# Clustered attention and dense layers: more buffers for the weight sums, recovery in a bank of its own, late weights on another queue

## The chip, the cores and the metric

The kernel runs on one core of a Trainium2 chip. The metric is the device time of the whole launch in microseconds, as the median of several runs. The engines are named PE (TensorE), DVE (VectorE), ACT (ScalarE), POOL (GpSimd) and SP (SyncE); SP and ACT also issue DMA transfers.

## The reference

```python
B, H, S, D = 4, 8, 768, 64               # 16 clusters for each head
q_assign = argmax(q_n @ c_n.T)           # q, k, centroids normalised
k_assign = argmax(k_n @ c_n.T)
scores = where(q_assign == k_assign, q @ k.T / 8, -1e9)
attn = softmax(scores) @ v               # in fp32
x = attn, heads joined                   # (4, 768, 512)
u = x + (x.T @ U @ V).T                  # U: 768 x 32, V: 32 x 768, mixes tokens
out = u + relu(u @ w_ch1) @ w_ch2        # 512 -> 2048 -> 512
```

U, V and the two weights come as 64-bit words, which hold numpy's float64; all else is fp32.

## The kernel before

There is one plan. Every piece of work is a Python function, `at(time, fn, ...)` gives it a place, and at the end the pieces are sorted by place and issued in that order; each engine executes its own instructions strictly in the order of issue (`keep_order`). A place is a number without unit. `M0` is the place at which the dense layers begin.

**Attention** (16 pairs of heads, 12 places each) comes first. It matters here only in that its last pairs, and the token mixing of the last batch (`mix_u`, `mix_sum`, `mix_v`), reach into the first places behind `M0`.

**Dense layers of batch 0**, places `M0` to `M0 + 32`: two halves of the tokens (`nh = 2`), 16 steps each. A step f is `gemm1` (12 matmuls into a bank `ps_h`), `after_gemm1` (ACT: Relu into `hh`, L605; DVE: the difference `hl`, L606) and `gemm2` (9 matmuls into three banks y). Each fp32 product is made of three products of high and low parts. The weights are in four groups of four steps, `wg[g]`.

**Loading weights** (`load_weights`, stages 0 to 3, eight steps a group; `stages` holds the places): `fetch` brings 64-bit words into one of two raw buffers (L151); `upper` (ACT, L159) and `join` (three DVE instructions, L169 to L172) turn them into fp32; stage 3 splits them into a high part (ACT, L190) and a low part (L191, on DVE in groups 2 and 3). Groups 2 and 3 are loaded during the first half of the dense layers, one step a place.

**Weight sums.** Batches 1 to 3 use a scheme with seven products instead of eight for 2 x 2 blocks, which needs four sums of weight blocks for each of eight pieces of the weights (n = 0 to 7: four groups, two matrices, one piece every 3.2 places from `M0 + 1.5`). `recover` adds low and high part again (ACT copies the low part into a bank `ps_r`, L652; DVE adds the high part and writes a temporary, L653); `combine` makes the four sums in place on POOL (L658 to L664); `split` divides each into high (ACT, L671) and low part (POOL, L672), in one of two buffers `o`; `store_sum` writes the buffer to DRAM, `wc` (L675). Unsummed blocks go there from the weights themselves (`store_block`, L642). Temporaries of pieces n and n + 1 lie in different places, except that 6 and 7 have the same one.

**Batches 1 to 3**, 28 places each: `seven1` and `seven2` do the seven products of the two matrices, with weights fetched back from `wc` (`fetch_w1` L762, `fetch_w2` L774); `after1`, `h_sums` and `h_halves` between them, `after2` behind (L875). Before a batch, `turn_half` transposes its tokens, `u_sums` (DVE, L748) makes four differences of token blocks, and `u_halves` (ACT L753 and L757, POOL L754 and L758) splits seven operands. After a batch, `join_up` adds the products together in eight additions of 768 columns (L902, DVE and POOL) and stores the output; these fall into the first places of the next batch.

**PSUM** in the dense stage: four banks in rotation for everything called with `work` (`ps_h`, the joins' `ps_t`, `ps_r`, transposes), and four more in the pool `ps_y`, in rotation too, three of which a half holds. In the seven-product stage `bank()` takes the two pools by turns.

All transfers but one kind go through SP's queue, which also executes in order and stands at a transfer until what it waits for is done.

Of the kernel before, what the change touches and what calls it, by code (L numbers as in the profile page):

```python
# [29 lines left out]
F32 = mybir.dt.float32  # L30
# [15 lines left out]
P = 128  # L46
# [50 lines left out]
    "mix":  (  3.36,   6.22,  15.04,  16.96),  # L97
    "g0":   ( 35.66,  38.22,  42.54,  52.94),
    "g1":   (-26.11, -21.73,  -20.5, -18.29),
    "g2":   (  -1.6,   -0.6,    0.3,    0.6),  # L100
    "g3":   (  6.25,    7.2,    8.1,    8.4),
}

spots = [0.66, -0.06, 1.8, 2.25, 1.26, 2.09, 2.97, 3, 3.49, 3.81, 4.58, 5.03]
# [13 lines left out]
def clustered_attention_moe(ctx: ExitStack, tc: tile.TileContext, qk, v, cen, moe_U, moe_V, w1, w2, out):  # L118
# [20 lines left out]
    def work(name):  # L139
        return ps_w.tile([P, 512], F32, name=name, tag="w")  # L140
# [2 lines left out]
    make_identity(nc, ident)  # L143
    u_scr = [dram.tile([P, NT, DM], F32, name=f"u_scr{b}") for b in range(B)]

    def fetch(srcs, n):

        step = srcs[0].shape[0]
        rw = raw.tile([P, 512], I64, name="rw")[0:step * len(srcs), 0:n]
        for i, src in enumerate(srcs):  # L150
            nc.sync.dma_start(out=rw[i * step:(i + 1) * step], in_=src)  # L151
        return rw

    def upper(rw):
# [23 lines left out]
    def load_weights(g, step, stage):  # L178

        k, i = divmod(step, 4)  # L180
        if stage == 0:
            parts[g, step] = fetch([(w1, w2)[k][g, :, i, :]], 512)
        elif stage == 1:
            parts[g, step] = upper(parts[g, step])
        elif stage == 2:
            parts[g, step] = join(*parts[g, step], g > 1)
        else:
            w = parts.pop((g, step))[2].bitcast(F32)
            hi, lo = wg[g][2 * k][:, i, :], wg[g][2 * k + 1][:, i, :]
            nc.scalar.copy(hi, w)  # L190
            (nc.vector if g > 1 or g == 1 and step in (1, 2, 3, 5) else nc.gpsimd).tensor_sub(lo, w, hi)  # L191
# [368 lines left out]
    def open_mlp():  # L560

        early.close()
        sb = pool["sb"] = ctx.enter_context(tc.tile_pool(name="msb", bufs=1, reuse_waits="tile"))
        pool["y"] = ctx.enter_context(tc.tile_pool(name="ps_y", bufs=4, space=PSUM, reuse_waits="tile"))
        wg[2].append(weight_tile(2, "w2l", sb))
        pool["u1"] = sb.tile([P, 2 * ND * HS], F32R, name="u1")
        turned[1] = [pool["u1"][:, k * ND * HS:(k + 1) * ND * HS].rearrange("p (d n) -> p d n", d=ND) for k in range(2)]
        pool["h"] = [sb.tile([P, 2, HS], F32R, name=f"hx{k}") for k in range(3)]
        pool["f"] = sb.tile([P, 2 * ND * S], F32, name="f")
# [38 lines left out]

    def gemm2(i, f):
        if f == 0:  # L610
            live["y", i] = [pool["y"].tile([P, 512], F32, name=f"y_{t}", tag="y") for t in range(HT)]
        y, (hh, hl) = live["y", i], live.pop(("h", i, f))
        _, _, w2h, w2l = wg[f // FG]
        for t in range(HT):
            ts = slice(t * P, (t + 1) * P)
            nc.tensor.matmul(y[t], hh[:, ts], w2h[:, f % FG, :], start=(f == 0), stop=False)
            nc.tensor.matmul(y[t], hh[:, ts], w2l[:, f % FG, :], start=False, stop=False)
            nc.tensor.matmul(y[t], hl[:, ts], w2h[:, f % FG, :], start=False, stop=(f == NF - 1))
# [26 lines left out]
    def temps(n):  # L645
        at = 3072 * (n % 2 == 0 or n > 5)
        return [pool["f"][:, at + 512 * j:at + 512 * j + 512].rearrange("p (a n) -> p a n", a=2) for j in range(4)]

    def recover(n, k, g, j):
        hi, lo = (blocks(k, g, part)[("A21", "A11", "A22", "A12")[j]] for part in range(2))  # L650
        ps = work("ps_r").rearrange("p (a n) -> p a n", a=2)
        nc.scalar.copy(ps, lo.bitcast(F32))  # L652
        nc.vector.tensor_add(temps(n)[j], ps, hi.bitcast(F32))  # L653

# [8 lines left out]
        else:  # L663
            nc.gpsimd.tensor_sub(f[3], f[3], f[2])  # L664

    def split(n, k, g, j):
        w = temps(n)[(1, 0, 2, 3)[j]]
        o = pool["f"][:, 5120:6144] if j % 2 else pool["f"][:, 2048:3072] if n < 6 else pool["rw"]
        o = live["o", n, j] = o.rearrange("p (a n) -> p a n", a=2)
        hi, lo = (o[:, :, part * 256:part * 256 + 256] for part in range(2))  # L670
        nc.scalar.copy(hi.bitcast(F32R), w)  # L671
        nc.gpsimd.tensor_sub(lo.bitcast(F32R), w, hi)  # L672

    def store_sum(n, k, g, j):
        nc.sync.dma_start(out=wc[k][g][:, :, slot[k][("S3", "S1", "S2", "S4")[j]], :], in_=live.pop(("o", n, j)))  # L675


    uc = {key: arena[:, 2 * XS + 1536 * s:2 * XS + 1536 * s + 1536].rearrange("p (h k n) -> p h k n", h=2, k=2)
          for s, key in enumerate(order[0])}
    w1s = [w0.rearrange("p k i n -> p (k i n)")[:, 3584 * k:3584 * k + 3584] for k in range(2)]  # L680
    spare, count = [], {"bank": 0, "f": 0}

    def pieces(x, n):
        return [x[:, k * n:(k + 1) * n] for k in range(x.shape[1] // n)]
# [4 lines left out]
    def open_sevens():  # L689

        pool["w2s"] = [[arena[:, 0:3584]], [arena[:, 3584:6144], wg[2][3].rearrange("p i n -> p (i n)")[:, 0:1024]]]
        pool["ys"] = [x.rearrange("p (d t n) -> p d t n", d=ND, t=2) for x in pieces(pool["f"], ND * S)]
        at_end = w0.rearrange("p k i n -> p (k i n)")[:, 7168:7936]
        spare.extend(pair(x) for x in (arena[:, 16896:17664], arena[:, 17664:18432], at_end,
                                       wg[2][3].rearrange("p i n -> p (i n)")[:, 1024:1792]))
        pool["st"] = rows.tile([P, HT, DM], F32, name="st", tag="R")
        ring = []
        for _ in range(2):
            pool["rw"] = raw.tile([P, 512], I64, name="rw").bitcast(F32)
            ring += pieces(pool["rw"][:, 0:768], HS)  # L700
        for _ in range(2):
            ring.append(raw.tile([P, 512], F32, name="rw_g")[:, 0:HS])
            ring.append(raw.tile([P, 512], I32, name="rw_t").bitcast(F32)[:, 0:HS])
        pool["ring"] = ring

    def free_rows():
        spare.extend(pair(x) for x in pieces(pool["u1"], 2 * HS))
# [11 lines left out]
    def ring():  # L719
        count["f"] += 1  # L720
        return pool["ring"][count["f"] % len(pool["ring"])]

    def bank():
        count["bank"] += 1
        ps = work("ps_p") if count["bank"] % 2 else pool["y"].tile([P, 512], F32, name="ps_q", tag="y")
        return ps[:, 0:HS]

    def fetch_half(b, h):
# [8 lines left out]
    def u_block(b, key):  # L737
        k, t = int(key[1]) - 1, int(key[2]) - 1
        return pool["ys"][1 - b % 2][:, 2 * k:2 * k + 2, t]

    def u_sums(b, key):

        live["t", key] = [ring() for _ in range(2)]
        for k, to in enumerate(live["t", key]):
            b11, b12, b21, b22 = (u_block(b, x)[:, k] for x in (B11, B12, B21, B22))
            one, two = {T1: (b12, b11), T3: (b12, b22), T2: (b22, live["t", T1][k]),
                        T4: (b21, live["t", T2][k] if key == T4 else None)}[key]
            nc.vector.tensor_sub(to, one, two)  # L748

    def u_halves(b, key):  # L750
        if key[0] == "B":
            hi, lo = uc[key][:, 0], uc[key][:, 1]
            nc.scalar.copy(hi, u_block(b, key))  # L753
            nc.gpsimd.tensor_sub(lo, u_block(b, key), hi)  # L754
        else:
            for k, x in enumerate(live["t", key]):
                nc.scalar.copy(uc[key][:, 0, k], x)  # L757
                nc.gpsimd.tensor_sub(uc[key][:, 1, k], x, uc[key][:, 0, k])  # L758

# [253 lines left out]
    for n_, (g, k) in enumerate((g, k) for g in range(NG) for k in range(2)):  # L1013
        c = M0 + 1.5 + 3.2 * n_
        for r in range(4):
            at(c + 0.4 * r, recover, n_, k, g, r)
            at(c + (0.9, 1.4, 1.75, 2.1)[r], combine, n_, r)
            at(c + (1.6, 2.0, 2.4, 2.8)[r], split, n_, k, g, r)
            at(c + (2.1, 2.5, 2.9, 3.3)[r], store_sum, n_, k, g, r)
        for r, name in enumerate(("A11", "A12", "A22")):  # L1020
            for half in range(2):
                x = 2 * r + half
                at((95 + 47 * k + 6 * x) if g == 0 else M0 + 1 + 4.1 * (n_ - 2) + 0.65 * x, store_block, k, g, name, half)

    at(M0 + 18, open_sevens)
    at(M0 + 31.3, free_rows)
# [2 lines left out]
    for b in range(1, B):  # L1029
        o = M0 + NF * nh + 28 * (b - 1)  # L1030
        if b == 1:
            fetched, turns, sums = (o - 13.9, o - 6.4), (o - 7.7, o - 5.4), o - 3.8
        else:
            fetched, turns, sums = (o - 20, o - 14), (o - 17.2, o - 9.7), o - 4.5
        for h in range(2):
            at(fetched[h], fetch_half, b, h)
            for d in range(ND):
                at(turns[h] + 0.4 * d, turn_half, b, h, d)
        at(sums - 0.45, u_halves, b, B11)
        for k, key in enumerate((T1, T2, T3, T4)):  # L1040
            at(sums + 0.25 * k, u_sums, b, key)
        for k, key in enumerate((T2, T3, T1, B21, T4, B22)):
            at(sums + 0.45 + 0.42 * k, u_halves, b, key)

        seq = [(1, 0), (1, 1), (1, 2), (2, 0), (1, 3), (2, 1), (1, 4), (2, 2), (1, 5), (2, 3),
               (1, 6), (2, 4), (1, 7), (2, 5), (2, 6), (2, 7)]
# [22 lines left out]
                for K in range(2):  # L1069
                    at(t + 7 * U + 0.01 * K, fetch_w2, (x - x % 2 + 2 + K) % 8, *slots)  # L1070
        if b < B - 1:
            for j in range(8):
                at(o + 28.4 + 0.65 * j, join_up, b, j)
    for K in range(2):
        for s0, s1 in ((0, 4), (4, 7)):
            at(M0 + 23 + K, fetch_w1, K, s0, s1)
# [35 lines left out]
```

## Time and profile before

| | |
|---|---|
| median of 3 runs | 1042.35 us (1042.16 to 1042.52) |
| the profiled execution | 1039.17 us, of which its span 1037.4 |
| PE busy | 963.4 us, 93% |
| DVE, POOL, ACT busy | 704.7, 620.7, 470.1 us |
| TensorE's granted clock, mean | 0.976 |
| DMA | 205.27 MB, mean 198 GB/s |
| dense layers of batch 0 | from 467 us to 660 us |

The rows of the profile name an engine, a line of the kernel, an operation and a tile. A row "A <- B" of the waits says that A sat idle until B released it: total us, times, longest. In the timeline a row is start, duration, engine, line, and in brackets the idle time before it with what ended it. In the windows, each engine's busy time in a stretch is followed by the granted clock (1.00 is full), the busy share of the DMA engines and the rate. A group of instructions has count, busy us, mean ns, and idle time before. SPq and ACTq are the queues that issue DMAs. Busy time of PE is modelled: matmuls overlap, so that a matmul's row is longer than the time until the next one starts.

### The profile page before, as it was taken

Reading aid. Unit: us, or ns where it says so; the run is one execution under the profiler, and the core shown is the slowest. Engines: PE = TensorE matmul, PEld = TensorE weight load, DVE = VectorE, ACT = ScalarE, POOL = GpSimd, SP = SyncE. Lnnn points to the kernel's source line nnn. Section 1 sums busy time; section 2 is a strip of 40 time slices with the busy share of each in tenths; the row PEclk is TensorE's granted clock in tenths of the full one; section 3 lists DMA queues with packets and bytes.
Section 4 is the critical chain, followed back from the end, with each engine's and each line's share of the span. In section 5 each row is a group of like instructions: output and inputs, shape, how many; then the busy total and the mean of one; then the engine's idle time right before and its main releaser. Section 6 shows DMA issues by size and latency. Waiting matters only on the chain.

```text
span 1037.4 us, 15318 instructions
## 1 busy us (share of the span) xinstructions
PE 963.4 (93%) x5368; PEld 786.2 (76%) x5368; DVE 704.7 (68%) x1298; ACT 470.1 (45%) x837; POOL 620.7 (60%) x477
## 2 busy tenths in 40 slices
PE   6999999999999999897877979999999999999997
PEld 3666665666667666556656768999999999999997
DVE  5797777777777766866667323565687656875767
ACT  4454654565556554553444343453333433334330
POOL 5467676888688877732444655653486533864431
PEclk9899999999999999998998999999999999999999
DMA  7754555656475635333887678577666876677743
GB/s 185 190 131 114 146 149 149 176 158 160 122 217 145 168 89 173 98 121 102 292 306 233 226 258 316 178 260 272 241 228 234 284 278 244 219 259 240 272 143 142
DMA packets 68028, 205.27 MB, mean 198 GB/s; under 512 B 8112, under 2 KB 25520, under 8 KB 63088
## 3 DMA queue, kind: packets, MB, share of 16 engines
q1 hardware_dynamic: 67568, 204.21, 62.2%
q8 instruction: 42, 0.69, 0.3%
q14 instruction: 34, 0.28, 0.1%
q10 hardware_dynamic: 384, 0.10, 0.0%
HBM read 131.07 MB, written 41.94 MB: 167 GB/s over the span
## 4 chain that ended last, share of the span: by engine, by line
PE 69%; DVE 13%; DMA 5%; issue 5%; ACT 4%; POOL 3%; SPq 0%; ACTq 0%; DVEq 0%; POOLq 0%
PE o_ps L487 11%; PE ps_max L440 7%; PE st L464 6%; PE st L466 5%; DMA wc<-f 3%; PE ps_q L855 2%; PE ps_q L857 2%; PE ps_q L856 2%; PE ps_p L791 2%; PE ps_p L793 2%; PE ps_p L792 2%; PE ps_q L793 2%; PE ps_q L792 2%; PE ps_q L791 2%; PE ps_p L855 2%
## 5 line engine op out<-in xcount | busy, mean ns | idle before, releaser
L479 POOL TENSOR_TENSOR T<-T,pr 128x768 f32<-128x768 f32 x120 | 226.6, 1888 | 46.2 <-ACT pr L469 19.3
L442 DVE TENSOR_REDUCE m<-ps_max 128x1 f32<-128x384 f32 x384 | 195.2, 547 | 82.6 <-PE ps_max L440 81.1
L469 ACT ACTIVATE pr<-st 128x768 f32<-128x768 f32 x192 | 154.4, 812 | 86.2 <-PE st L466 68.3
L487 PE MATMUL o_ps<-pr,vt 128*64 128x384 f32 x768 | 133.4, 498 | 0.1
L440 PE MATMUL ps_max<-arena 128*128 128x384 f32 x384 | 127.6, 383 | 6.3 <-DVE oh L356 2.5
L464 PE MATMUL st<-arena 128*128 128x384 f32 x384 | 105.3, 356 | 1.8 <-ACT pr L469 1.8
L440 PEld LDWEIGHTS ps_max<-arena 128*128 128x128 f32 x384 | 71.1, 193 | 44.9 <-issue 21.4
L487 PEld LDWEIGHTS o_ps<-pr,vt 128*64 128x64 f32 x768 | 53.1, 139 | 67.1 <-issue 60.8
L466 PE MATMUL st<-arena 97*128 97x384 f32 x384 | 99.9, 342 | 4.3 <-DMA arena<-mT 2.4
L479 POOL TENSOR_TENSOR T<-pr 128x768 f32<-128x768 f32 x30 | 56.5, 1884 | 64.9 <-ACT pr L469 64.9
L464 PEld LDWEIGHTS st<-arena 128*128 128x128 f32 x384 | 66.4, 190 | 17.7 <-issue 9.9
L466 PEld LDWEIGHTS st<-arena 97*128 97x128 f32 x384 | 70.6, 191 | 6.2 <-issue 4.5
L491 ACT COPY os<-o_ps 128x384 f32<-128x384 f32 x32 | 15.3, 479 | 105.8 <-PE o_ps L487 105.8
L791 PE MATMUL ps_p<-arena,w 128*128 128x384 f32 x178 | 59.9, 336 | 3.2 <-ACT ring L803 3.2
L672 POOL TENSOR_TENSOR f<-f 128x512 fp32r<-128x512 f32 x28 | 36.0, 1285 | 44.0 <-ACT f L671 42.1
L793 PE MATMUL ps_p<-arena,w 128*128 128x384 f32 x178 | 59.5, 334 | 0.0
L792 PE MATMUL ps_p<-arena,w 128*128 128x384 f32 x178 | 59.5, 334 | 0.0
L791 PE MATMUL ps_q<-arena,w 128*128 128x384 f32 x158 | 53.5, 339 | 0.0
L792 PE MATMUL ps_q<-arena,w 128*128 128x384 f32 x158 | 52.9, 334 | 0.0
L793 PE MATMUL ps_q<-arena,w 128*128 128x384 f32 x158 | 52.8, 334 | 0.0
L606 DVE SCALAR_TENSOR_TENSOR hx<-ps_h,hx 128x384 fp32r<-128x384 f32 x32 | 17.7, 552 | 46.9 <-ACT hx L605 46.9
L380 POOL TENSOR_TENSOR arena<-R,arena 128x768 fp32r<-128x768 f32 x18 | 34.5, 1924 | 13.2 <-ACT arena L375 7.6
(482 smaller groups left out, 2441.5 us busy)
## 6 DMA issues: line engine op xcount, KB each, us to landing
w<-wc SPq DMA_DIRECT2D x24, 1024.0 KB
w<-wc SPq DMA_DIRECT2D x24, 768.0 KB
rw<-in_w SPq DMA_DIRECT2D x32, 512.0 KB
wc<-f SPq DMA_DIRECT2D x28, 512.0 KB
arena<-wc SPq DMA_DIRECT2D x17, 768.0 KB
R<-in_qk SPq DMA_DIRECT2D x32, 384.0 KB
arena<-arena SPq DMA_DIRECT2D x32, 384.0 KB
arena<-arena SPq DMA_DIRECT2D x64, 192.0 KB
```

The lines of the kernel that those rows point to most:

```text
L440: nc.tensor.matmul(ps[:, 0:HS], x1[:, 0, g // 2, g % 2, t * P:(t + 1) * P], x1[:, 1, h, g % 2, :], start=True, stop=True)
L442: nc.vector.reduce_max(live["m2", i][:, h, u:u + 1], ps[:, 0:HS], axis=AX.X)
L464: nc.tensor.matmul(st[:, j, 0:HS], x1[:, 1, hk, j, ks], x1[:, 0, h, j, :], start=True, stop=False)
L466: nc.tensor.matmul(st[:, j, 0:HS], x2[0:97, 1, hk, j, ks], x2[0:97, 0, h, j, :], start=False, stop=True)
L469: nc.scalar.activation(pr, st[:, :, 0:HS], AF.Exp, scale=SCALE)
L479: eng.tensor_add(T, live["p", i, h, 0] if c == 1 else T, live["p", i, h, c])
L487: nc.tensor.matmul(o_ps[64 * j:64 * j + 64, 0:HS], vv[:, c, j, :], pr[:, j, :], start=(c == 0), stop=(c == NT - 1))
L672: nc.gpsimd.tensor_sub(lo.bitcast(F32R), w, hi)
L791: nc.tensor.matmul(ps, w[:, 0, k], u[:, 0, k], start=(k == 0), stop=False)
L792: nc.tensor.matmul(ps, w[:, 0, k], u[:, 1, k], start=False, stop=False)
L793: nc.tensor.matmul(ps, w[:, 1, k], u[:, 0, k], start=False, stop=(k == 1))
L855: nc.tensor.matmul(ps, w[:, 0], h[:, 0], start=(j == 0), stop=False)
```

## The change

Sums: `split` becomes `split_high` and `split_low`. The high part goes to one of six places of 512 columns in rotation (four for the last two pieces); two of the six are the buffers `rw_t` of the loading. The low part is written over the sum in its temporary. `store_sum` becomes two transfers, of high and low part, with rows of 256 values instead of 512. Their places move back by 0.3 to 0.4 or so. `recover` has a bank of its own, `ps_r`, as the fourth of the pool `ps_y`, whose banks are now named and no longer in rotation.

Loads: the weights of groups 2 and 3 are fetched on ACT's queue, the places of their stages change by a few tenths, and the blocks of group 1 are stored from `M0 - 9` and `M0 - 2.5` on, before from `M0 + 1` and `M0 + 5.1`.

Batches: `u_sums` makes one difference at a time, with places of their own, `u_halves` likewise; the eight additions of `join_up` move from 0.4 to 4.95 places (one every 0.65) to two at 0.02 and 0.1 and six from 5 to 5.9.

```diff
-    "g2":   (  -1.6,   -0.6,    0.3,    0.6),
-    "g3":   (  6.25,    7.2,    8.1,    8.4),
+    "g2":   ( -1.25,      0,    0.4,    0.7),
+    "g3":   (  6.75,      8,    8.4,    8.7),
...
-            nc.sync.dma_start(out=rw[i * step:(i + 1) * step], in_=src)
+            queue.dma_start(out=rw[i * step:(i + 1) * step], in_=src)
...
-            parts[g, step] = fetch([(w1, w2)[k][g, :, i, :]], 512)
+            parts[g, step] = fetch([(w1, w2)[k][g, :, i, :]], 512, nc.scalar if g > 1 else nc.sync)
...
-        pool["y"] = ctx.enter_context(tc.tile_pool(name="ps_y", bufs=4, space=PSUM, reuse_waits="tile"))
+        pool["y"] = ctx.enter_context(tc.tile_pool(name="ps_y", bufs=1, space=PSUM, reuse_waits="tile"))
+        pool["o"] = [raw.tile([P, 512], I32, name="rw_t").bitcast(F32) for _ in range(2)]
...
-            live["y", i] = [pool["y"].tile([P, 512], F32, name=f"y_{t}", tag="y") for t in range(HT)]
+            live["y", i] = [pool["y"].tile([P, 512], F32, name=f"y_{t}") for t in range(HT)]
...
+    def high_of(n, j):
+        f = pool["f"]
+        places = [f[:, 5120:5632], f[:, 5632:6144], *pool["o"], f[:, 2048:2560], f[:, 2560:3072]]
+        count["o"] += 1
+        return places[count["o"] % (6 if n < 6 else 4)].rearrange("p (a n) -> p a n", a=2)
...
-        ps = work("ps_r").rearrange("p (a n) -> p a n", a=2)
+        ps = pool["y"].tile([P, 512], F32, name="ps_r").rearrange("p (a n) -> p a n", a=2)
...
-    def split(n, k, g, j):
+    def split_high(n, j):
         w = temps(n)[(1, 0, 2, 3)[j]]
-        o = pool["f"][:, 5120:6144] if j % 2 else pool["f"][:, 2048:3072] if n < 6 else pool["rw"]
-        o = live["o", n, j] = o.rearrange("p (a n) -> p a n", a=2)
-        hi, lo = (o[:, :, part * 256:part * 256 + 256] for part in range(2))
-        nc.scalar.copy(hi.bitcast(F32R), w)
-        nc.gpsimd.tensor_sub(lo.bitcast(F32R), w, hi)
+        o = live["o", n, j] = high_of(n, j)
+        nc.scalar.copy(o.bitcast(F32R), w)
+
+    def split_low(n, j):
+        w = temps(n)[(1, 0, 2, 3)[j]]
+        nc.gpsimd.tensor_sub(w.bitcast(F32R), w, live["o", n, j])
 
     def store_sum(n, k, g, j):
-        nc.sync.dma_start(out=wc[k][g][:, :, slot[k][("S3", "S1", "S2", "S4")[j]], :], in_=live.pop(("o", n, j)))
+        to = wc[k][g][:, :, slot[k][("S3", "S1", "S2", "S4")[j]], :]
+        nc.sync.dma_start(out=to[:, :, 0:256], in_=live.pop(("o", n, j)))
+        nc.sync.dma_start(out=to[:, :, 256:512], in_=temps(n)[(1, 0, 2, 3)[j]])
...
-        ps = work("ps_p") if count["bank"] % 2 else pool["y"].tile([P, 512], F32, name="ps_q", tag="y")
+        tag = ("y_2", None, "ps_r", None, "y_0", None, "y_1", None)[count["bank"] % 8]
+        ps = pool["y"].tile([P, 512], F32, name="ps_q", tag=tag) if tag else work("ps_p")
...
-            at(c + (1.6, 2.0, 2.4, 2.8)[r], split, n_, k, g, r)
-            at(c + (2.1, 2.5, 2.9, 3.3)[r], store_sum, n_, k, g, r)
+            at(c + (1.9, 2.25, 2.6, 2.8)[r], split_high, n_, r)
+            at(c + (2.4, 2.7, 3.0, 3.3)[r], split_low, n_, r)
+            at(c + (2.8, 3.1, 3.4, 3.7)[r], store_sum, n_, k, g, r)
...
-                at((95 + 47 * k + 6 * x) if g == 0 else M0 + 1 + 4.1 * (n_ - 2) + 0.65 * x, store_block, k, g, name, half)
+                since = (95, 142, M0 - 9, M0 - 2.5)
+                at(since[n_] + (6 if g == 0 else 0.9) * x if g < 2 else M0 + 1 + 4.1 * (n_ - 2) + 0.65 * x,
+                   store_block, k, g, name, half)
...
-        at(sums - 0.45, u_halves, b, B11)
         for k, key in enumerate((T1, T2, T3, T4)):
-            at(sums + 0.25 * k, u_sums, b, key)
-        for k, key in enumerate((T2, T3, T1, B21, T4, B22)):
-            at(sums + 0.45 + 0.42 * k, u_halves, b, key)
+            for r in range(2):
+                at((o - 4.9 if b > 1 else o - 3.9) + (k + 0.5 * r) * (1 if b > 1 else 0.8), u_sums, b, key, r)
+        for key, when_ in ((B11, -4.95), (T1, -4.2), (B21, -3.7), (T2, -3.2), (B22, -2.7), (T3, -2.2), (T4, -1.2)):
+            at(o + when_ * (1 if b > 1 else 0.8), u_halves, b, key)
...
-            for j in range(8):
-                at(o + 28.4 + 0.65 * j, join_up, b, j)
+            for j, when_ in enumerate((0.02, 0.1, 5, 5.3, 5.1, 5.45, 5.6, 5.9)):
+                at(o + 28 + when_, join_up, b, j)
```

Here `o` is the place at which batch b begins; before, `sums` was `o - 3.8` for batch 1 and `o - 4.5` for the others.

More of the change, by code (lines that the diff above doesn't have):

```diff
@@ L144, in clustered_attention_moe, with fetch @@
     u_scr = [dram.tile([P, NT, DM], F32, name=f"u_scr{b}") for b in range(B)]
-    def fetch(srcs, n):
+    def fetch(srcs, n, queue=nc.sync):
         step = srcs[0].shape[0]
@@ L680, in clustered_attention_moe @@
     w1s = [w0.rearrange("p k i n -> p (k i n)")[:, 3584 * k:3584 * k + 3584] for k in range(2)]
-    spare, count = [], {"bank": 0, "f": 0}
+    spare, count = [], {"bank": 0, "f": 0, "o": 0}
     def pieces(x, n):
@@ L698, in open_sevens @@
         for _ in range(2):
[L699 to L704, printed above, removed]
+            ring += pieces(raw.tile([P, 512], I64, name="rw").bitcast(F32)[:, 0:768], HS)
+        ring += [raw.tile([P, 512], F32, name="rw_g")[:, 0:HS] for _ in range(2)]
+        pool["ring"] = ring + [x[:, 0:HS] for x in pool["o"]]
     def free_rows():
@@ L739, in u_block, with u_sums @@
         return pool["ys"][1 - b % 2][:, 2 * k:2 * k + 2, t]
[L741 to L748, printed above, removed]
+    def u_sums(b, key, k):
+        to = live["t", key, k] = ring()
+        b11, b12, b21, b22 = (u_block(b, x)[:, k] for x in (B11, B12, B21, B22))
+        one, two = {T1: (b12, b11), T3: (b12, b22), T2: (b22, live["t", T1, k]),
+                    T4: (b21, live["t", T2, k] if key == T4 else None)}[key]
+        nc.vector.tensor_sub(to, one, two)
     def u_halves(b, key):
@@ L755, in u_halves @@
         else:
-            for k, x in enumerate(live["t", key]):
+            for k in range(2):
+                x = live["t", key, k]
                 nc.scalar.copy(uc[key][:, 0, k], x)
@@ L1031, in clustered_attention_moe @@
         if b == 1:
-            fetched, turns, sums = (o - 13.9, o - 6.4), (o - 7.7, o - 5.4), o - 3.8
+            fetched, turns = (o - 13.9, o - 6.4), (o - 7.7, o - 5.4)
         else:
-            fetched, turns, sums = (o - 20, o - 14), (o - 17.2, o - 9.7), o - 4.5
+            fetched, turns = (o - 20, o - 14), (o - 17.2, o - 9.7)
         for h in range(2):
```

## The prediction

> **What bounds the kernel now.** I read the windows by stage first, then the starts of the hidden-layer matmuls in the timeline, then the chain and the waits of each half of that stage. Attention ends at 467 us; from there to about 660 the first batch goes through the dense layers (32 steps of `gemm1` and `gemm2`), while weights of groups 2 and 3 are loaded and the 32 weight sums are built; after 660 three batches run in the seven-product form.
>
> ```profile
> span 1037.4 us, 15318 instructions
> core 0: us, PE busy (x) PEld busy (x) DVE busy (x) ACT busy (x) POOL busy (x), PEclk, DMA share, GB/s
> 467.00:572.00 105.00, 82.76 (x376) 68.17 (x377) 71.33 (x118) 47.93 (x95) 44.79 (x36) 0.93 0.69 230
> 572.00:660.00 88.00, 77.16 (x382) 68.45 (x381) 27.88 (x42) 31.20 (x63) 52.73 (x41) 0.96 0.70 245
> 507.00:522.00 15.00, 12.42 (x57) 10.13 (x58) 12.84 (x21) 7.75 (x16) 8.91 (x7) 1.00 0.86 298
> 467.03 0.44 PE L597 MATMUL ps_h<-arena,w 128*128 128x384 f32 x1 [0.24 <-DVE arena L589]
> 591.79 0.33 PE L597 MATMUL ps_h<-u,arena 128*128 128x384 f32 x1
> 595.98 0.33 PE L597 MATMUL ps_h<-u,arena 128*128 128x384 f32 x1
> ```
>
> The first L597 row is the first matmul of step 0, and the windows are cut where step 0, step 16 and the end of step 31 fall. The other two rows are the first matmuls of steps 20 and 21: an undisturbed step takes 595.98 - 591.79 = 4.19 us, so 16 steps would take 67.0. The first sixteen took 105, the other sixteen 88. The windows' busy time of PE hides much of this, since it counts matmuls at a slow clock as busy. No engine is full: DVE 71.33 of 105, DMA 0.69.
>
> What stands between is seen in the longest pieces of the chain of each half, and in who waited for whom there:
>
> ```profile
> 515.09 4.66 DMA wc<-f
> 537.90 4.39 DMA wc<-f
> 557.78 5.33 DMA wc<-f
> 579.05 5.10 DMA wc<-f
> 593.65 4.03 DMA wc<-f
> 607.57 10.40 DMA wc<-f
> ...
> ACT f L671 <- DMA wc<-f: 16.7, 8, 4.2
> ACT rw_g L159 <- DMA rw<-in_w: 20.3, 7, 5.2
> PE ps_h L597 <- DVE f L653: 6.6, 3, 3.3
> ...
> ACT f L671 <- DMA wc<-f: 24.1, 5, 9.2
> DVE hx L606 <- ACT hx L605: 42.8, 10, 8.7
> PE ps_uT L734 <- DVE f L653: 6.4, 1, 6.4
> ...
> SPq L151 <- DVE ps_t L172: 43.7, 12, 9.9
> ```
>
> `split` (L671) has two buffers for hi and lo together; ACT, which executes in order, stands at L671 until the store from two sums ago has landed. Behind it in ACT's order is the Relu of L605, behind that DVE's L606, behind that `gemm2`. That is the whole tie: a store's landing time, which nothing needs, sets the pace of PE. PE also stands for DVE's L653, because `recover` takes its banks from the same four as the hidden layer. The last row is the sync queue (SP), standing at a weight load until the join two steps earlier has freed the raw buffer, with stores queued behind it.
>
> **The change part by part.**
>
> *Six high buffers, low part in place.* The instructions stay: 32 ACT copies, 32 POOL subtractions of the same 512 columns. A high buffer returns after six sums instead of two, and the store is 3.9 places of the plan behind it, some 3.9 x 6.6 = 26 us at today's pace (105/16 = 6.6), against a longest wait of 10.40: the ACT wait is gone. The low part now lies in the temporary, so `recover` of the next set but one waits for a store; that is 3.3 places, 22 us, later at the least, so it too is covered, except for set 7, which has the same temporaries as set 6. There DVE's L653 at place 23.9 stands for stores issued from 23.5 to 24.4, the last two behind the fetch of the second chunk of w1 on SP. Bounds: 0 to 10.40 (the row at 607.57, where such fetches stood ahead of a store); I take half, 5.2, since the fetch of the first chunk now goes out ahead of all stores of set 6. Behind that DVE add stands L606 of steps 24 and 25, and behind it PE.
>
> First half: the three store pieces, 4.66 + 4.39 + 5.33 = 14.4 us. Bounds: 0, if what is late next is as late; and what DVE allows. DVE does the same work afterwards, 71.33 us, and its best stretch (12.84 of 15, 0.86) would need 71.33/0.86 = 82.9, so 22.1 is the most. I take 14.4: by the counts below DVE is what is late next, and it leaves no more than a few us beyond.
>
> ```profile
> L169 DVE TENSOR_SCALAR ps_t<-rw_g 128x512 int32<-128x512 int32 x16 | 10.9, 682 | 0.0
> L170 DVE SCALAR_TENSOR_TENSOR ps_t<-rw_g,ps_t 128x512 int32<-128x512 int32 x16 | 11.1, 696 | 0.6
> L172 DVE SCALAR_TENSOR_TENSOR ps_t<-rw,ps_t 128x512 int32<-128x512 int32 x16 | 11.1, 696 | 0.5
> L191 DVE TENSOR_TENSOR w1l<-ps_t,w1h 128x512 fp32r<-128x512 f32 x4 | 2.8, 692 | 7.7 <-ACT w1h L190 7.6
> L653 DVE TENSOR_TENSOR f<-ps_r,arena 128x512 f32<-128x512 f32 x12 | 8.1, 683 | 7.2 <-ACT ps_r L652 7.2
> L606 DVE SCALAR_TENSOR_TENSOR hx<-ps_h,hx 128x384 fp32r<-128x384 f32 x16 | 8.8, 550 | 4.1 <-ACT hx L605 4.1
> L672 POOL TENSOR_TENSOR f<-f 128x512 fp32r<-128x512 f32 x28 | 36.0, 1285 | 44.0 <-ACT f L671 42.1 <-DVE hx L606 1.8
> ```
>
> Per step of the first half DVE does a join, a low part, a Relu difference and 4/3.2 = 1.25 recoveries: 0.682 + 0.696 + 0.696 + 0.692 + 0.550 + 1.25 x 0.683 = 4.17 us, just what PE needs for a step. POOL does 2.5 operations of 1.285 a step, 3.2 us, and has room.
>
> Second half: the pieces are 5.10 + 4.03 + 10.40 = 19.5, less the 5.2 of set 7, 14.3. But PE can't gain what it didn't lose: it idled 88 - 77.16 = 10.8 us, of which I leave a little over one to waits that stay, and its clock was 0.96, at most 0.04 x 88 = 3.5 more. So 9.5 to 13.0 is the room, 0 the other end; I take 9.5 and half of 3.5, 11.2.
>
> *A bank of its own for recovery.* `recover` leaves the four shared banks, so that `gemm1` no longer waits for L653: 6.6 us in the first half and 6.4 in the second, but these overlap the chain pieces above and are not added again. Its price: ACT's copy waits each time for DVE's add of the one before. The plan puts them 0.4 place, 1.7 us at 4.19 a place, apart, and copy and add need less, so 0 unless DVE is behind; the other end is the slower rival. The dense output has three fixed banks instead of four in rotation; `gemm2` of the second half begins two steps' pieces after the sums are read, so 0.
>
> *Late weights through ScalarE's queue.* Sixteen loads leave SP for ACT, 1.25 places ahead of their use instead of 1.
>
> ```profile
> L151 SPq DMA_DIRECT2D rw<-in_w x32: 327/334/1372, 107.4 to 556.5; - x32
> L217 ACTq DMA_DIRECT2D arena<-mT x18: 677/732/1286, 24.1 to 434.5; - x18
> L675 SPq DMA_DIRECT2D wc<-f x28: 512/513/1549, 492.3 to 638.3; - x28
> ```
>
> Issuing costs ACT 16 x 0.327 = 5.2 us at least and 16 x 0.732 = 11.7 at most (the only rows of ACT's queue), beside 105 - 47.93 = 57 idle: 0. The load's wait for the join of two steps ago is now in ACT's order, but L190, which needs the same join, stands right ahead of it, so it holds nothing longer: 0. The gain is that stores on SP no longer stand behind it, and that loads no longer stand behind stores. ACT stood 20.3 us for loads; if all that went, the first half would reach DVE's limit of 22.1 and the sum below would be 1001.9. The page "DMA: Bandwidth & Descriptors" of the Trainium skill (Issuing engines are not separate DMA queues) speaks against this: all issuing engines' transfers run on the same 16 DMA engines, and another queue saves only time on the sequencer; by it the 14.4 stands and with it 1009.6. The row of the busy stretch, DMA 0.86 at 507 to 522, points the same way, and I take nothing for faster loads.
>
> *Stores in two pieces.* SP issues 32 more, 32 x 0.513 = 16 us over 193: hidden. Bytes are the same, the rows half as long. Two bounds: a row costs by its bytes, 0; or by its number, which is a rival below. Six to nine stores of group 1's blocks move ahead of 467 us, where DMA has room: a little better, 0.
>
> *Differences and joins spread.* At the two later batch borders PE waits thus (all of 657 to 1037, five groups):
>
> ```profile
> PE ps_p L791 <- ACT ring L803: 3.2, 2, 1.6
> PE ps_p L855 <- DVE f L875: 2.5, 2, 1.2
> PE ps_q L855 <- DVE f L875: 2.2, 2, 2.0
> PE ps_q L855 <- ACT acc L873: 1.9, 1, 1.9
> PE ps_q L855 <- DVE acc L875: 0.9, 2, 0.5
> ...
> L902 DVE TENSOR_TENSOR f<-f,acc 128x768 f32<-128x768 f32 x12 | 13.3, 1131 | 0.1
> ```
>
> Together 10.7 us. The 1.6s, the 2.0 and the 1.9 (7.1) come in the first three products of a batch, where DVE has about 12 operations of L606's size, 0.55, in each 7 us and four joins of some 1.1 on top. Six of the eight joins now come at 5 to 5.9 places, where second products begin and DVE has four adds instead of twelve. The other 3.6 come where the differences of the tokens stand in a row ahead of L875; these are spaced out. Bounds: 10.7, or below nothing, if joins bunched in 0.9 place delay the adds there by their 4 x 1.1 twice, -9. I take 7.1, the joins' share.
>
> **The sum.** 14.4 + 11.2 + 7.1 = 32.7 us off the span of 1037.4. The profiled execution took 1039.17 in all, the median of the runs is 1042.35, 3.2 above it; against the median the forecast is 1042.35 - 32.7 = 1009.6.
>
> **The rivals.**
>
> *More, as all ties go.* First half to DVE's 82.9 (22.1), second with its clock (13.0), both borders clean (10.7): 45.8, so 996.5. For it: the recovery bank gives PE two steps of lead. Against: 86% was DVE's best in 15 us, not in 80. On the clock, the row below shows a matmul of 0.54 us, where the same took 0.33 at 591.79, after 2.82 us of standing. "TensorE: Matmul & The Clock Gate" of the Trainium skill (What's actually happening) has the clock halved after some 3.4 us idle; the trace agrees (0.93, 0.96 in these windows), and by it fewer gaps give the time twice.
>
> ```profile
> 478.51 0.54 PE L597 MATMUL ps_h<-arena,w 128*128 128x384 f32 x1 [2.82 <-DVE f L653]
> ```
>
> *DMA becomes the bound.* If a half row costs as much as a whole one, 18 stores of the first half add 18 x 0.52 MB at 230/0.69 = 333 GB/s, 28 us, to 0.69 x 105 = 72: 100 of 105, a gain of 5 at most; 14 stores add 21 to 62 in the second: 83 of 88, again 5. With the borders 17, so 1025. Against it is a stretch with more than half its packets under 2 KB, which moved 294/0.805 = 365 GB/s:
>
> ```profile
> DMA packets 2167, 2.94 MB, mean 294 GB/s; under 512 B 125, under 2 KB 1379, under 8 KB 2166
> ...
> q1 hardware_dynamic: 2166, 2.94, 80.5%
> ```
>
> *Slower: the single recovery bank.* If DVE is behind, ACT's next copy stands for the add of the one before, and with ACT stand Relu and joins. The price is a join (2.07 us) at each of the 20 recoveries of the first half, 41 us: 1051. It decides from 32.7/20 = 1.6 us a recovery. For it: DVE's 4.17 in a step of 4.19, and bursts of four. Against: ACT has 57 idle us to catch up, and PE has a step in hand.
>
> *Nothing comes of it.* The store wait moves from ACT to DVE's L653 in every set, not set 7 alone: about 1042. Against: 22 us of distance.
>
> **How the numbers follow.** Forecast 0.48 (its own range 1000 to 1019), more 0.17, DMA-bound 0.20, nothing 0.05, slower 0.10. A measurement here tells about 0.2%, 2 us, from no change. Faster 0.85, same 0.05, slower 0.10. The range 990 to 1033 takes the forecast and nearly all of the two cases beside it.
>
> **What would show it.** Right: no ACT wait for `wc` stores left but some at the end; L606's wait for L605 under 15 us; steps of 4.3 to 5.5 us; DVE over 80% in the first half; one wait of L653 for a store near step 24; L803's wait at the borders gone. Wrong: ACT's copy for recovery waiting for L653 over 1 us on the mean, DMA share near 1.0 with lower GB/s, loads still awaited 20 us, or new waits of L875 behind joins at 5 places.

## The result, and the profile after

| | before | after |
|---|---|---|
| median | 1042.26 us | 1025.18 us (1025.03 to 1025.75) |
| ratio | | 0.9837, 95% interval 0.982 to 0.9854 |
| span of the profiled execution | 1037.4 us | 1024.0 us |
| step 0 to step 16 of the dense stage | 105.1 us | 92.7 us |
| step 16 to the first product of batch 1 | 83.9 us | 75.9 us |
| from there to the end | 381.3 us | 388.3 us |

The change makes the kernel 17 us faster, 1.6%. By the spans of the two profiled executions it is 13.4 us: that of before lay 3.1 us below its median, that of after 0.6 above. By these spans the dense stage gives 12.4 + 8.0 = 20.4 us, and batches 1 to 3 take 7.0 of it back. The cuts are these matmuls of the timeline: step 16 and the first product of batch 1 in before (step 0 is at 467.03), then step 0, step 16 and the first product in after. Batch 1 begins at 656.08 in the kernel before, not at 660.

```profile
572.16 0.34 PE L597 MATMUL ps_h<-u,w 128*128 128x384 f32 x1
656.08 0.34 PE L791 MATMUL ps_p<-arena,w 128*128 128x384 f32 x1
```

```profile
467.14 0.45 PE L598 MATMUL ps_h<-arena,w 128*128 128x384 f32 x1 [0.23 <-DVE arena L590]
559.80 0.34 PE L598 MATMUL ps_h<-u,w 128*128 128x384 f32 x1
635.68 0.34 PE L799 MATMUL ps_p<-arena,w 128*128 128x384 f32 x1
```

The windows of after, cut there (columns as in the windows of before):

```profile
467.00:560.00 93.00, 80.20 (x378) 64.95 (x379) 68.77 (x114) 47.19 (x92) 43.78 (x35) 0.96 0.73 238
560.00:636.00 76.00, 72.59 (x362) 63.99 (x361) 31.09 (x45) 32.56 (x65) 54.44 (x42) 0.98 0.81 284
636.00:1024.00 388.00, 367.26 (x2073) 362.60 (x2071) 264.51 (x469) 140.13 (x302) 190.39 (x173) 0.98 0.65 231
```

The waits of the dense stage of after (line numbers have moved, and move by one or so between the runs: here L606 is the Relu, L607 its difference, L659 recovery's copy, L660 its add, L676 the copy of the high part):

```profile
DVE hx L607 <- ACT hx L606: 27.2, 13, 7.5
ACT ps_r L659 <- DVE f L660: 22.3, 16, 8.3
...
DVE f L660 <- DMA wc<-f: 12.3, 3, 8.0
...
ACT rw_g L159 <- DMA rw<-in_w: 4.8, 2, 3.8
...
ACT rw_t L676 <- DMA wc<-f: 0.9, 1, 0.9
```

ACT's 16.7 + 24.1 + 9.2 us of waiting for stores have become 0.9, and its 20.3 for raw words 4.8. DVE's new wait for stores is there, in three pieces. In the DMA columns, the first half moves 238/0.73 = 326 GB/s at full share against 230/0.69 = 333 before, the second 284/0.81 = 351 against 245/0.70 = 350: with the stores in rows of half the length the rate fell by about 2% in one half and not at all in the other.

The waits of PE behind 630 us are the surprise:

```profile
PE ps_q L863 <- DVE rw L838: 6.1, 2, 3.0
PE ps_q L863 <- DVE ring L838: 4.0, 2, 2.0
PE ps_q L863 <- DVE rw_t L838: 3.9, 3, 2.0
PE ps_p L863 <- DMA arena<-wc: 1.1, 2, 0.6
```

The five groups at the borders of before are all gone, as forecast. In their place `seven2` (L863) stands for `h_sums` (L838), 14.0 us in seven waits, in all three batches and also in batch 1, where no joins fall. One of them in the timeline, with a later piece of what follows:

```profile
729.46 0.44 PE L863 MATMUL ps_q<-u,arena 128*128 128x384 f32 x1 [3.03 <-DVE rw L838]
...
731.07 0.67 PE L863 MATMUL ps_q<-h,arena 128*128 128x384 f32 x1
731.54 0.52 PE L864 MATMUL ps_q<-h,arena 128*128 128x384 f32 x1
```

Some 1.6 us after the wait of 3.03 us matmuls of the same shape take 0.52 to 0.67 us instead of 0.34: the wait is paid for again in clock. This holds for four of the seven. Windows of 3.3 to 3.4 us behind the waits of 1.98, 3.03, 2.04 and 3.03 us have a clock of 0.50; behind the other wait of 2.00 us, and those of 0.68 and 1.20, it stays at 1.00. The last of the four, and the 2.00:

```profile
860.40:863.70 3.30, 3.30 (x11) 3.20 (x12) 1.09 (x2) 0.34 (x1) 0.17 (x1) 0.50 0.02 5
828.00:831.40 3.40, 3.40 (x20) 3.40 (x21) 2.04 (x5) 0.98 (x2) 3.04 (x4) 1.00 0.00 0
```

Four such stretches at half clock lose about 4 x 3.4 x 0.5 = 6.8 us.

`h_sums` reads three results of `seven1` straight from their PSUM banks, late in the plan. A product that gets such a bank has to wait for it. In the kernel before, the second pool of banks hands out the bank whose last use comes first in the plan; in the programs' own bank numbers that pool begins batch 1 with 2, 1, 0, 3, 2, 3, 1, 0, 2, 3. The changed kernel names the banks, and `bank()` takes them in the cycle 3, 0, 1, 2 throughout, whether they are still to be read or not.

### The profile page after: what moved, and what is told of

Read it like the earlier page. It is cut to its first block, busy times and chain, and to the rows that moved or that the text cites. A ratio compares the mean times of both kernels' runs of the same rounds, so it can differ in the third digit from the quotient of the medians.

```text
span 1024.0 us, 15360 instructions
## 1 busy us (share of the span) xinstructions
PE 962.9 (94%) x5368; PEld 785.0 (77%) x5368; DVE 709.2 (69%) x1298; ACT 471.5 (46%) x837; POOL 624.1 (61%) x477
## 5 line engine op out<-in xcount | busy, mean ns | idle before, releaser
L849 POOL TENSOR_TENSOR h<-ring,h 128x384 fp32r<-128x384 f32 x21 | 21.5, 1031 | 36.0 <-ACT h L848 19.5
L607 DVE SCALAR_TENSOR_TENSOR hx<-ps_h,hx 128x384 fp32r<-128x384 f32 x32 | 17.7, 553 | 27.4 <-ACT hx L606 27.2
## 6 DMA issues: line engine op xcount, KB each, us to landing
w<-wc SPq DMA_DIRECT2D x24, 1024.0 KB
arena<-wc SPq DMA_DIRECT2D x10, 1024.0 KB
```

## The experiments

Theory A: the fixed cycle of named banks takes back what the rest brings. Its rival: the new places of differences and joins delay `h_sums`. Theory B, for the dense stage: the store wait of two buffers, and PE's wait for recovery's banks, set its pace, and the queue of the loads is worth nothing. Its rivals give the gain to one of these alone, or to the queue. Ratios are to the kernel before on the same chip, with 95% intervals. The runs were spread over several chips, on which the median of the kernel before was 1039.4 to 1042.3 us, so between chips the ratios are the better comparison. Code cuts are shortened.

**e1_rotating: the pool in rotation again, everything else changed.**

```diff
-tile_pool(name="ps_y", bufs=1, ...)
+tile_pool(name="ps_y", bufs=4, ...)        # y, ps_r and ps_q all with tag="y"
-        tag = ("y_2", None, "ps_r", None, "y_0", None, "y_1", None)[count["bank"] % 8]
+        ps = work("ps_p") if count["bank"] % 2 else pool["y"].tile(..., name="ps_q", tag="y")
```

> The changed kernel with one thing put back: the four banks of ps_y (three dense outputs, recovery, every second product of batches 1 to 3) are one pool in rotation again, which hands out the bank that the plan releases first, instead of four named banks in a fixed cycle. Theory (the fixed cycle is where the gain went: seven waits of L863 for L838, 6.1 + 4.0 + 3.9 = 14.0 us, and the half clock that follows them): these waits go and nothing else moves, the part behind the first L799 falls from 388.3 us to some 371 to 374, 1009 to 1012 us in all. Rival (the new places of differences and joins cost the time, by delaying the sums L838): the waits of L863 for L838 stay, 1022 to 1026.

Measured: 1005.86 us, 0.9676 (0.9652 to 0.9699). The part behind the first product takes 1003.4 - 634.6 = 368.8 us, 19.5 less than in the changed kernel and 12.5 less than before; the dense stage is as it was (92.9 and 74.3). All waits of PE in that part, and its window:

```profile
PE ps_q L862 <- DVE f L882: 1.8, 2, 1.6
PE ps_q L862 <- ACT acc L880: 1.2, 1, 1.2
PE ps_p L862 <- DMA arena<-wc: 0.4, 1, 0.4
```

```profile
635.00:1003.00 368.00, 359.32 (x2072) 356.64 (x2070) 256.52 (x469) 139.97 (x302) 192.03 (x173) 1.00 0.68 244
```

The waits for `h_sums` are gone, the clock is 1.00. Waits fell by 11.7 us (15.1 to 3.4), the time by 19.5; the other 7.8 are what 388 us at 0.98 instead of 1.00 come to, and the four stretches at half clock are 6.8 of them. The gain is more than the theory's 1009 to 1012. By the ratios (0.9837 to 0.9676) it is 17 us.

**e2_named_alone: the kernel before with named banks and nothing else.**

```diff
-        ps = work("ps_p") if count["bank"] % 2 else pool["y"].tile([P, 512], F32, name="ps_q", tag="y")
+        tag = ("y_2", None, "y_3", None, "y_0", None, "y_1", None)[count["bank"] % 8]
+        ps = pool["y"].tile([P, 512], F32, name="ps_q", tag=tag) if tag else work("ps_p")
```

> The kernel before with one thing of the change alone: the four banks of ps_y are named and go round in a fixed cycle; recovery still takes its bank from the shared four. Theory (the fixed cycle costs the time): waits for h_sums (L830 in the kernel before, L832 or so here) of about 14 us appear in batches 1 to 3 beside the 10.7 us that are there, 1053 to 1060 us. Rival (places of differences and joins): no such waits, 1041 to 1044.

Measured: 1054.17 us, 1.0144 (1.0122 to 1.0167). Its waits of PE behind 655 us begin thus, above those of before:

```profile
PE ps_q L856 <- DVE rw L831: 6.1, 2, 3.0
PE ps_q L856 <- DVE rw_t L831: 5.0, 3, 2.4
PE ps_q L856 <- DVE ring L831: 4.0, 2, 2.0
PE ps_p L792 <- ACT ring L804: 3.2, 2, 1.6
```

Seven waits again, 15.1 us, without any of the new places, and 1.4% or 15 us more time. With e1 this settles A. Its dense stage is that of before but for the names of the banks, and that of e3 is the same code; the first half takes 108.1 us here and 108.6 in e3, against 105.1 in the profile of before. So this half varies by some 3 us between executions.

**e3_spread_alone: the kernel before with the new places of differences, splits and joins** (the last two hunks of the diff and `u_sums` for one half at a time).

> The kernel before with one part of the change alone: the places of the token differences, of the operand splits and of the joins. Theory (they do what was forecast, and the loss lies elsewhere): the 10.7 us of waits at the two later borders go, with some us of half clock behind them, 1029 to 1035 us. Rival (the new places cost more than they bring): 1042 to 1050.

Measured: 1029.64 us, 0.9909 (0.9882 to 0.9935). From the first product (657.94) to the end (1026.5) 368.6 us, 12.7 less than before; of the waits at the borders 2.6 us are left.

**e8_old_joins: as e1, the joins at their old places.**

```diff
-            for j, when_ in enumerate((0.02, 0.1, 5, 5.3, 5.1, 5.45, 5.6, 5.9)):
+            for j, when_ in enumerate(0.4 + 0.65 * x for x in range(8)):
```

> As e1_rotating, but with the eight joins at 0.4 to 4.95 places as before; the differences stay spread. Theory (the joins bring about two thirds of what the borders gained): waits of some 7 us of the kind 'L798 for L810' and 'L862 for L882' return, 1013 to 1017. Rival (the differences bring it): under 3 us, 1005 to 1008.

Measured: 1013.56 us, 0.9753 (0.9718 to 0.9788), about 7.7 us above e1. The three waits of before that were put down to the joins are back:

```profile
PE ps_p L798 <- ACT ring L810: 3.2, 2, 1.6
PE ps_q L862 <- DVE f L882: 2.2, 2, 2.0
PE ps_q L862 <- ACT acc L880: 1.9, 1, 1.9
```

**e4_rotating_sp_loads: as e1, the late weights on SP's queue.** In `load_weights`, `nc.sync` for all groups.

> As e1_rotating, but the weights of groups 2 and 3 are loaded through SP's queue again, at the new places. Theory (the other queue only takes the loads out of SP's order; loads and stores share the engines that move them): ACT's waits for raw words rise from 4.8 us towards the 20.3 of before, the first sixteen steps are 0 to 6 us longer than with ACT's queue, 1009 to 1017 in all. Rival (the queue is what brought the first half its 12 us): over 10 us longer, 1019 to 1025.

Measured: 1003.27 us, 0.9656 (0.9631 to 0.9681), the same as e1 within the intervals. ACT's wait for raw words is 4.1 us, not towards 20. So with the new places either queue brings the loads in time, and that part of the expectation was wrong.

**e7_old_load_places: as e4, and the stages of the loads at their old places too.**

> As e4_rotating_sp_loads, but with the places of the load stages of groups 2 and 3 as before the change too, so that nothing of the change to the loads is left. Theory (loads were late only because ACT and the stores held them): within 4 us of e4, 1000 to 1008. Rival (the new places are needed to have the raw words in time): ACT waits over 10 us for raw words, 1010 or more.

Measured: 1001.94 us, 0.9637 (0.9601 to 0.9674), again the same. But ACT's wait for raw words is large:

```profile
ACT rw_g L159 <- DMA rw<-in_w: 34.0, 12, 6.8
```

The rival's wait came and its time did not. The wait is larger than before the change (20.3), though stores no longer hold ACT: it was the longer lead of the new places, 1.25 instead of 1, that had cured it in e4. e12 asks whether it costs anything.

**e5_shared_bank: as e1, recovery in the four shared banks again.** In `recover`, `ps = work("ps_r")`.

> As e1_rotating, but recovery takes its bank from the four shared ones again, as before the change. Theory (both parts carry the dense stage: the buffers free ACT, the bank frees PE): waits of L598 for L660 of 6 to 14 us return, mostly in the first sixteen steps, with half clock behind them, 1010 to 1020 us. Rival (the buffers alone carry it): 1004 to 1008.

Measured: 1012.23 us, 0.9735 (0.9687 to 0.9783), 6 us above e1, though the two intervals overlap a little. The first sixteen steps take 100.0 us instead of 92.9, the other sixteen 75.5 instead of 74.3. PE's first three waits there; the one for L660 is below the 6 to 14 us that the theory gave it:

```profile
PE ps_h L598 <- DVE hx L607: 6.1, 2, 4.2
PE ps_h L598 <- DVE f L660: 4.2, 2, 2.8
PE ps_h L598 <- DVE u L590: 3.8, 1, 3.8
```

**e6_two_buffers: as e1, two high buffers** (`places[count["o"] % 2]`).

> As e1_rotating, but with two high buffers instead of six; low parts stay in the temporaries, recovery keeps its bank. Theory (the wait of ACT for the store of two sums ago set the pace): L676 waits for stores again, 25 to 50 us in all, the 32 steps are 8 to 20 us longer, 1014 to 1026. Rival (the bank of recovery alone carries the dense stage): under 5 us longer, 1004 to 1010.

Measured: 1006.02 us, 0.9686 (0.9647 to 0.9726). This tested nothing: at the new places the plan issues the third copy before the first store, so that the buffer is overwritten and ACT waits only 1.0 us for stores at L676 (two high parts in four are not what gets stored). The next pair puts it right.

**e9_six_early and e10_two_early: as e7, with copies, subtractions and stores at the places of before, and six or two high buffers.** In both, a low part is written over a sum that the third combination still reads, so that two of the four sums are others; instructions and transfers are the same.

```diff
-            at(c + (1.9, 2.25, 2.6, 2.8)[r], split_high, n_, r)       # low 2.4 to 3.3, store 2.8 to 3.7
+            at(c + (1.6, 2.0, 2.4, 2.8)[r], split_high, n_, r)        # low the same, store 2.1 to 3.3
-        return places[count["o"] % (6 if n < 6 else 4)]...
+        return places[count["o"] % 2]...                               # e10 alone
```

> As e7_old_load_places, with the six high buffers, but the copy, the subtraction and the stores of the sums at the places they had before the change (1.6 to 2.8 and 2.1 to 3.3), so that a store precedes the copy two sums later. The control for e10. Both theories: within 6 us of e7, 998 to 1008.

> As e9_six_early, but with two high buffers. In this order a copy does wait for the store of two sums ago, which e6 did not have. Theory (that wait set the pace of the dense stage): ACT waits 25 to 50 us for stores, 8 to 20 us longer than e9. Rival (with recovery in its own bank PE is far enough ahead, and the buffers bring nothing): within 4 us of e9.

Measured: e9 1000.78 us, 0.9622 (0.9605 to 0.9639); e10 1012.74 us, 0.9739 (0.9718 to 0.9759). ACT's longest group of waits in e10's dense stage:

```profile
ACT f L676 <- DMA wc<-f: 40.8, 11, 7.2
```

It has none in e9. The wait is as large as L671's in `f` before the change (16.7 + 24.1), and it costs 12 us. The two halves of the stage are 95.0 and 79.6 us in e10, 90.5 and 73.0 in e9: 4.5 us in the first, 6.6 in the second.

**e11_later_fetch: as e7, the second fetch of w1 behind the stores of set 6.** `fetch_w1` at `M0 + 23 + 1.8 * K`.

> As e7_old_load_places, but the second fetch of w1 goes to 24.8 places, behind the four stores of set 6, before 24. Theory (that fetch makes DVE wait for set 6's low parts, and PE loses some us by it in steps 24 to 27): L660's wait for stores falls from 11.5 us to under 6, those steps are 1 to 4 us shorter, 997 to 1002. Rival (PE has a step in hand there and loses nothing; or the later fetch is missed at the start of batch 1): 1000 to 1006.

Measured: 1004.97 us, 0.9663 (0.9644 to 0.9682). L660's wait fell only from 11.5 to 7.4 us, and steps 24 to 27 were no shorter. A miss: the time is the rival's.

**e12_longer_lead: as e7, with a lead of 1.45 to 1.55 places from the fetch of raw words to their use, by a later use.**

```diff
-    "g2":   (  -1.6,   -0.6,    0.3,    0.6),
-    "g3":   (  6.25,    7.2,    8.1,    8.4),
+    "g2":   ( -1.55,      0,    0.4,    0.7),
+    "g3":   (  6.25,    7.7,    8.1,    8.4),
```

> As e7_old_load_places, but the raw words are fetched 1.45 to 1.55 places ahead of their use (fetch at -1.55 and 6.25, first use at 0 and 7.7), on SP's queue. Theory (ACT's 34 us of waits for raw words hold the Relus and cost PE its 7.9 us of waits L617 for L606): those waits fall under 15 us, the first sixteen steps are 2 to 6 us shorter, 995 to 1000. Rival (DVE's own work, 68 us in those steps, sets their pace, and ACT's waits are slack): within 2 us of e7, 1000 to 1004.

Measured: 995.58 us, 0.9571 (0.9545 to 0.9597): the fastest here, 2.7% better than the changed kernel (1025.18 us, 0.9837), on SP's queue alone. ACT's wait for raw words, and the dense stage:

```profile
ACT rw_g L159 <- DMA rw<-in_w: 3.4, 2, 2.7
```

```profile
466.00:551.00 85.00, 75.92 (x377) 62.25 (x377) 68.77 (x114) 46.40 (x90) 43.27 (x34) 1.00 0.75 235
551.00:625.00 74.00, 71.10 (x360) 62.39 (x359) 31.25 (x45) 33.26 (x66) 54.49 (x43) 1.00 0.89 313
```

In e7 and e4 the first of these was longer, at another clock:

```profile
466.00:557.00 91.00, 80.72 (x377) 65.14 (x378) 68.11 (x114) 45.69 (x90) 43.35 (x34) 0.94 0.71 226
466.00:558.50 92.50, 80.75 (x377) 65.71 (x378) 68.61 (x114) 46.98 (x92) 43.69 (x34) 0.94 0.72 231
```

Against e7 the first half is 5.9 us shorter (90.7 to 84.8), and 0.06 of 91 us is 5.5: the gain looks like one of clock. PE's waits for the Relu (L617 for L606) fell from 7.2 to 2.9 us, all its waits there from 10.2 to 8.9. That ACT's waits for raw words were the cause isn't shown: in e4 they were 4.1 us, nearly as short as here, and its first half took 92.3. Nor does the clock alone order the times, for e9's first half took 90.5 us at 0.92, e10's 95.0 at 0.95. The gain stands; its cause is open.

## Why the prediction was right, and where it was wrong

The forecast was a gain of 32.7 us; 17 came. That is inside the range, but slower than the likeliest case's own range (1000 to 1019); the range reached so far only for the sake of the DMA-bound case, which didn't occur. By the spans, where 13.4 came:

| | forecast | measured |
|---|---|---|
| first half of the dense stage | 14.4 | 12.4 |
| second half | 11.2 | 8.0 |
| batches 1 to 3 | 7.1 | -7.0 |

Of the 19.3 us between the two columns, 14.1 are one term of the wrong sign.

*The step that failed* is the sentence on the banks: "The dense output has three fixed banks instead of four in rotation; ... so 0." It looked at the dense output alone. The same hunk turns `bank()` in every second of its 352 calls from a pool that avoids occupied banks into a fixed cycle; that edit was not costed, nor was any cover named for it. e1 prices it at 17 (by ratio) to 19.5 us (by the traces) beside the other parts, e2 at 15 alone. With that edit put back the kernel stands at 0.9676 of before, 1008.5 us on the chip of the forecast, 1.1 from the 1009.6.

*First half: the sum about right, its parts not.* The 14.4 us were the store wait's, and nothing was added for the bank of recovery, as overlapping with it. But two high buffers instead of six cost only 4.5 us of this half (e10 against e9), and the shared bank 7.1 (e5 against e1). Together that is 11.6 of the 12.4 measured, so the two hardly overlapped: one term was too large, another left out, and that the sum came near is in part luck. These are differences of single traces, and this half varied by 3 us without a change to it. DVE's limit of 82.9 us was not reached; e12 comes nearest with 84.8 us (551.04 - 466.26), DVE busy for 0.81 of it, and no run shows what stops it there.

*Second half: 3 us too much.* The window ended at 660, but the first product of batch 1 had started at 656.08, so this half took 83.9 us, not 88. That didn't hurt the sum, since PE was busy all through the 4 us between: from 572 to 656 it was busy for 73.16 of 84 us, and so idled the same 10.8. What was too small is the rest that stays. In the changed kernel PE still idles 76 - 72.59 = 3.4 us, where a little over one was left to such waits, and its busy time fell by 0.6 us, where 1.7 was taken for the clock. Other runs came further: 74.3 us in e1 and e12, 73.0 in e9. The buffers were worth 6.6 us here (e10 against e9), the bank 1.1 (e5 against e1). The term of 5.2 us for set 7 was there as a DVE wait (12.3 us), but e11, which shortened that wait by 4.1 us, brought no time.

*Borders: right, and too small.* e3 shows 12.7 us where 7.1 was taken of 10.7 waited. The waits fell by 8.1 (10.7 to 2.6); the rest is about what the clock gives, 0.99 in this part before and 1.00 in e3. The joins alone make 7.7 (e8).

*The queue: right to take nothing.* e4 shows no difference from e1. The rule of the Trainium skill, "DMA: Bandwidth & Descriptors" (Issuing engines are not separate DMA queues), held here: 1003.27 us on one queue, 1005.86 on two. The loads' lateness was cured by the longer lead (e4, e7), which the case of 1001.9 had ascribed to the queue. Issuing cost ACT 0.334 us a load, near the lower of the two bounds.

*The signs.* Of those named for being right, ACT's waits for stores and L803's waits at the borders went. L607 still waits 27.2 us for L606 (under 15 was named), DVE was busy for 0.74 of the first half (over 0.80), a step of that half took 5.8 us on the mean (4.3 to 5.5), and L660 waited three times for stores, not once. So the first half was less relieved than the forecast had it.

*The rivals.* "DMA becomes the bound" gave 1025, very near the measured time, for a reason that is refuted: the rate at full share fell by about 2% in one half of the stage and not in the other, and e1 has the same short rows at 1006. "Slower by the single recovery bank" did not occur. ACT did wait 22.3 us for L660, 1.4 us for each of 16 waits and 0.7 for each of 32 recoveries, but e5 shows the bank as a gain. A hit of the range on these grounds is luck.

## What to carry to other kernels

When an edit gives names to buffers that came from a rotating pool, list every other user of the pool, and ask in which order they were handed out and which of them are read late; here a fixed cycle cost about half of what the rest of the change brought. When a wait of an in-order engine is removed, look for the engine behind it in the order, not at the waiting engine's busy share. And price waits of PE at more than their length until the granted clock says otherwise: here 11.7 us of them brought 19.5 (e1), and 8.1 brought 12.7 (e3), 1.6 times as much.

## What the runs showed of the hardware

In batches 1 to 3 of the changed kernel, four of seven PE waits were followed by some 3.4 us at half clock: those of 1.98, 2.04 and twice 3.03 us, but not one of 2.00. A wait's length alone doesn't decide it here: in the first half of the dense stage, PE's wait of 2.24 us for L550 was followed by a clock of 0.50 in e1 (508.9 to 512.2), and one of 2.25 us for the same line by 1.00 in e12 (505.3 to 508.7). "TensorE: Matmul & The Clock Gate" of the Trainium skill (What's actually happening) names some 3.4 us of idling; here 3.03 us was followed by matmuls of 0.52 us instead of 0.34, and 1.98 us was enough once. Writing 1 KB rows instead of 2 KB left the DMA rate at full share as it was within about 2% (326 and 351 GB/s against 333 and 350).
